# Unread products ahead of and between PE's first four transposes, orders planned anew, and a last output tile in two halves

## The chip, the core and the metric

The kernel runs on one core of one Trainium2 chip. The metric is the device time of one execution in microseconds (us). The engines are called PE (matrix products, with PEld for its weight loads), DVE (vector), ACT (scalar), POOL and SP; DMA transfers are issued from the queues of SP, ACT and POOL. PE writes into eight banks of 128 x 512 fp32 sums, called `acc` here.

## The reference

```python
# attention: q, k, v are [8, 8, 576, 64]; bias_table is [32, 8]
scores = (1/sqrt(64)) * q @ k^T + bias_table[bucket(|i - j|)]
attn   = exp(scores - max) / sum
x      = (attn @ v), heads side by side          # [4608, 512]
# feed-forward
h   = x @ w_in                                   # w_in [512, 2048]
g   = h + sin(alpha * h)**2 / (alpha + 1e-9)
out = g @ w_out                                  # w_out [2048, 512], out [4608, 512] fp32
```

## The kernel before, in words

There are eight batch elements t of 576 tokens, with eight heads each, taken as four pairs p. For each element, PE makes transposed scores (tasks `T t.p.wh`: query half w, key half h; `R`, `L` and `S` hold the rest rows and tail keys of several pairs at once), ACT takes their exponential (L1228, L1233, L1192), and DVE multiplies the part near the diagonal by the exponential of the bias (the "band", L1256, L1238, L1242, L1198), which is held as a Toeplitz array `toep`. PE then forms `attn @ v` with a column of ones for the sums (`av`, L1266 and L1276), DVE divides (`norm`, L1286, L1287), and the result is transposed into `xT`: by PE and a copy for element 0 (`turn_x`, L1300, copies `x0.p.w`), by DMA for the others.

k and q of elements 0 and 1 (and q of element 2) come in natural layout and are transposed on PE with an identity: 64-column tiles, two side by side ("cols" shape). Pair 0 of element 0 comes in four pieces (k and q, half 0 and 1), each loaded in fp32, cast (L991, L993), transposed (`turn_half`, L1135, six transposes) and copied (`half_copy`, L1145, L1147). The other pairs come by DMAs on POOL's queue and are transposed whole (`turn`, L1155, twelve transposes; copies L1163 on ACT, L1165 on DVE). All products that use 64 of 128 rows ("rows"), 64 of 128 columns ("cols"), or both ("quad") are different tile shapes of PE; the rest are "full".

The bias goes through a small product with the table (`bias_sub`, L1075), an exponential (L1079), four products (`bias_mm`, L1088), a copy (`bias_copy`, L1093) and then DMAs that write `toep` (L1103); POOL's `mask` copies follow.

The feed-forward part is cut into nine blocks of 480 to 576 tokens and 16 units each: four products (`in b.f`, L1325), a sine on ACT (L1332), a square on ACT (L1337) or DVE (L1339), and the sum on DVE (L1353). The 36 output tiles of 128 tokens are made in pairs of tiles, each of 16 products with w_out (`mo`, L1368), evicted by a copy on ACT (L1305) or DVE (L1307), and stored by SP (L1378), 256 KB each. Some of the `mo` work is done in the "rows" shape (`OPT["rows"]`), to stand next to score products without a change of shape.

Every piece of work is a `_Task` with an engine and an assumed duration. `_graph` (L425) makes them, and `_Plan.run` (L182) walks them in time. The order of each engine is fixed by hand-over: `LINE` (L361) lists task numbers, engine by engine, and each engine takes its tasks in exactly that order. `OPT["scalar"]` names the copies, squares and evictions that go to ACT instead of DVE. `_Plan.filled` (L311) can put products that nobody reads (`fill`, L1124, into a free bank, from the array `blank` of ones) ahead of the k-th PE task, spread from 1.1 us or the task before; `FILLS` is empty before the change, so none are made. The planner's durations for PE are those at full pace throughout.

POOL's queue takes its loads in order: a load that waits (for instance `load_vt` of element 2, which waits until element 0's `av` products have read the buffer) holds all behind it.

Of the kernel before, what the change touches and what calls it, by code (L numbers as in the profile page):

```python
# [10 lines left out]
F32 = mybir.dt.float32  # L11
# [89 lines left out]
class _Task:  # L101
    __slots__ = ("eng", "dur", "emit", "deps", "prio", "lat", "take", "seq", "sn", "name",
                 "m_in", "m_out", "pipe", "pkt", "flow", "start", "end", "idx", "got", "wait", "low", "alt")

    def __init__(self, eng, dur, emit, deps=(), prio=0.0, lat=0.0, take=(), seq=None, name="",
# [9 lines left out]
        self.low = 8  # L115
        self.alt = None
# [3 lines left out]
class _Plan:  # L120
    HOP = 0.06
    LAT = {"PE": 0.17, "ACT": 0.1, "DVE": 0.09, "POOL": 0.1}
    SWITCH = {"PE": 0.096, "ACT": 1.3}
    START = (0.5, 2.0)
# [57 lines left out]
    def run(self):  # L182
# [23 lines left out]
        while n:  # L206
            moved = False
            nxt = None
            for e, cand in pool.items():
# [61 lines left out]
                dur = t.dur  # L271
                if t.m_in is not None:
                    if mode.get(e, t.m_in) != t.m_in:
                        dur += self.SWITCH[e]
                    if t.m_in != t.m_out:
                        dur += self.SWITCH[e]
                    mode[e] = t.m_out
# [83 lines left out]
LINE = """  # L361
# [57 lines left out]
"""  # L419


FILLS = ()


def _graph(K, opt):  # L425
# [74 lines left out]
    for g in range(4):  # L500
        b_mm.append(add("PE", 0.35, None, deps=[b_sel] + b_mm[:1], prio=opt["p_bias"],
                        take=[] if g else [(1, s_users)]))
        b_mm[g].emit = lambda g=g: K.bias_mm(g, tag(b_mm[0]))
# [927 lines left out]
```

## Time and profile before

| | us |
|---|---|
| runs | 382.05, 381.51, 380.55 (median 381.51) |
| profiled execution | 382.92 |
| its span | 381.1 |
| first transpose on PE (L1135) | 4.56 |
| first exponential of scores (L1228) | 7.67 |
| first band product on DVE (L1256) | 18.36 |
| first feed-forward product (L1325) | 35.00 |
| last copy of an output tile (L1305) | 377.53 to 378.13 |

Times of instructions are from the start of the span. A row of instructions in order of time has its start, its length, engine, line, operation, output <- inputs and count, and in brackets the idle time of the engine before it with what ended that. A row of the chain of waits has start, length and what ran. A row of a group ends with busy time, mean ns of one, and idle time before.

### The profile page before, as it was taken

The page shows a single profiled execution, that of the slowest core. Times are in us where ns is not written, and L with a number is a line of the kernel's source. Part 1 is how long each engine was busy: PE and PEld are TensorE (multiplying, and loading weights), DVE is VectorE, ACT ScalarE, POOL GpSimd, SP SyncE. Part 2 cuts the span into 40 slices and gives each one's busy share as a digit, 9 for nine tenths or more (in the row PEclk, how much of TensorE's full clock was granted, in tenths as well). Part 3 has the DMA queues.
Part 4 walks back from the last instruction along what each step waited for, and adds up shares of the span by engine and source line. Part 5 has one row for each costly group of instructions (what it writes and reads, how often), then busy time and mean ns, then how long its engine had stood idle before and what let it go on. Part 6 is the DMA issues. An engine that isn't in the chain of part 4 may idle for free.

```text
span 381.1 us, 9520 instructions
## 1 busy us (share of the span) xinstructions
PE 369.9 (97%) x3939; PEld 201.3 (53%) x3939; DVE 268.3 (70%) x635; ACT 314.2 (82%) x419; POOL 88.2 (23%) x105
## 2 busy tenths in 40 slices
PE   4999999999999999999999999999999999999996
PEld 3566445756454556464655465546655545444442
DVE  4686988949964996579748974696569869668402
ACT  4788999899999999999999899997998686557311
POOL 8874651180028201910000008300000000000000
PEclk9999999999999999999999999999999999999999
DMA  8999999499939996997392049941710110210005
GB/s 158 203 157 153 176 186 125 81 148 148 173 82 147 162 158 82 183 157 167 43 182 79 3 96 154 108 67 23 160 58 17 37 37 19 72 57 3 0 2 220
DMA packets 148172, 40.82 MB, mean 107 GB/s; under 512 B 134416, under 2 KB 143456, under 8 KB 148128
## 3 DMA queue, kind: packets, MB, share of 16 engines
q0 software_dynamic: 96656, 18.45, 61.0%
q1 hardware_dynamic: 50768, 21.22, 27.8%
q8 instruction: 31, 0.51, 0.6%
q10 hardware_dynamic: 704, 0.53, 0.6%
q14 instruction: 13, 0.11, 0.1%
HBM read 36.94 MB, written 15.93 MB: 139 GB/s over the span
## 4 chain that ended last, share of the span: by engine, by line
PE 86%; DVE 5%; ACT 3%; DMA 3%; issue 1%; POOL 1%; ACTq 0%; POOLq 0%
PE acc L1368 31%; PE acc L1325 29%; PE acc L1276 10%; PE acc L1220 8%; PE acc L1266 3%; DVE g L1353 2%; ACT u L1228 2%; PE acc L1155 2%; DMA v<-in_v_dram 2%; DMA xT<-in_k_dram 2%; PE acc L1179 2%; PE acc L1210 1%; PE acc L1184 1%; DVE s L1339 1%; DVE xp L1287 1%
## 5 line engine op out<-in xcount | busy, mean ns | idle before, releaser
L1368 PE MATMUL acc<-w_out,g 128*128 128x512 f16 (+1 forms) x744 | 148.0, 378 | 0.6 <-DVE touched L1173 0.5
L1325 PE MATMUL acc<-xT,w_in 128*128 128x512 f16 (+2 forms) x640 | 134.7, 358 | 0.1
L1228 ACT ACTIVATE u<-acc 128x1024 f16<-128x1024 f32 x128 | 123.6, 1038 | 8.0 <-PE acc L1220 6.9
L1332 ACT ACTIVATE s<-acc,alphaT 128x512 f16<-128x512 f32 (+2 forms) x144 | 94.1, 684 | 24.4 <-PE acc L1325 18.2
L1353 DVE SCALAR_TENSOR_TENSOR g<-s,inv_a,acc 128x512 f16<-128x512 f16 (+4 forms) x176 | 107.5, 647 | 9.5 <-ACT s L1337 7.9
L1325 PEld LDWEIGHTS <-w_in 128*128 128x128 f16 x640 | 58.0, 98 | 66.1 <-issue 2.3
L1368 PEld LDWEIGHTS <-g 128*128 128x128 f16 (+1 forms) x744 | 51.2, 96 | 50.7 <-issue 8.4
L1256 DVE TENSOR_TENSOR u<-u,toep 128x1024 f16<-128x1024 f16 (+1 forms) x128 | 59.1, 487 | 26.6 <-ACT u L1228 26.5
L1035 POOL DMA_DIRECT2D v<-in_v_dram x32 | 33.3, 1116 | 91.8 <-PE acc L1276 85.1
L1220 PE MATMUL acc<-qT,kT 64*128 64x256 f16 x512 | 48.1, 285 | 0.5 <-DVE kT L1165 0.5
L1276 PE MATMUL acc<-v,u 128*128 128x65 f16 x1024 | 45.6, 195 | 0.1
L1337 ACT ACTIVATE s<-s 128x512 f16<-128x512 f16 (+2 forms) x70 | 43.2, 630 | 1.2
L1276 PEld LDWEIGHTS <-u 128*128 128x128 f16 x1024 | 41.5, 99 | 4.2 <-issue 0.2
L1307 DVE COPY outs<-acc 128x512 f32<-128x512 f32 x27 | 18.4, 687 | 27.7 <-PE acc L1368 27.2
L1339 DVE TENSOR_TENSOR s<-s 128x512 f16<-128x512 f16 (+2 forms) x74 | 30.2, 419 | 10.2 <-ACT s L1332 10.2
L1220 PEld LDWEIGHTS <-kT 64*128 64x128 f16 x512 | 22.0, 96 | 28.7 <-issue 16.3
L1287 DVE TENSOR_TENSOR xp<-acc,rden 128x256 f16<-128x256 f32 (+1 forms) x64 | 31.4, 491 | 2.4
L1266 PE MATMUL acc<-vt,ut 128*128 128x130 f16 x128 | 28.6, 224 | 0.0
L1041 POOL DMA_DIRECT2D vt<-in_v_dram x16 | 13.3, 832 | 51.8 <-PE acc L1179 27.3
L1305 ACT ACTIVATE outs<-acc 128x512 f32<-128x512 f32 x9 | 5.3, 603 | 18.4 <-PE acc L1368 18.4
L1228 ACT ACTIVATE ut<-acc 128x1024 f16<-128x1024 f32 x16 | 16.5, 1029 | 2.6 <-PE acc L1179 2.0
L1286 DVE RECIPROCAL rden<-acc 128x4 f32<-128x4 f32 (+1 forms) x64 | 11.8, 185 | 9.6 <-PE acc L1276 9.2
(70 smaller groups left out, 231.7 us busy)
## 6 DMA issues: line engine op xcount, KB each, us to landing
out_dram<-outs SPq DMA_DIRECT2D x36, 256.0 KB, 2.5
v<-in_v_dram POOLq DMA_DIRECT2D x32, 128.0 KB, 7.4
staged_k<-in_k_dram POOLq DMA_DIRECT2D x6, 576.0 KB, 11.1
staged_q<-in_q_dram POOLq DMA_DIRECT2D x5, 576.0 KB, 12.9
w_in<-in_moe_w_in_dram POOLq DMA_DIRECT2D x4, 512.0 KB, 8.8
w_out<-in_moe_w_out_dram POOLq DMA_DIRECT2D x4, 512.0 KB, 10.1
xT<-in_q_dram POOLq DMA_DIRECT2D x11, 144.0 KB, 6.5
xT<-in_k_dram POOLq DMA_DIRECT2D x7, 144.0 KB, 6.2
```

Of the source, the lines that this page charges most:

```text
L1220: self.nc.tensor.matmul(out=s[:, o:o + 256], lhsT=self.kT[t % 2][r, p, 128 * c:128 * c + 128], rhs=self.qT[t % 2][r, p, 256 * w:256 * w + ...
L1228: self.nc.scalar.activation(out=c["u"], in_=c["s"], func=AF.Exp, scale=0.125)
L1256: self.nc.vector.tensor_tensor(out=io, in0=io, in1=m, op=ALU.mult)
L1266: nc.tensor.matmul(out=c["av"][:, 130 * j:130 * j + 130], lhsT=tail, rhs=vt[:, p, :], start=True, stop=True, skip_group_check=True)
L1276: nc.tensor.matmul(out=c["av"][:, 130 * j + 65 * a:130 * j + 65 * a + 65], lhsT=l, rhs=vv[:, ch, 2 * p + a, 0:65], start=False, stop=True, ...
L1287: self.nc.vector.tensor_tensor(out=self.ap(x, 256 * w, [[64, n], [1, 64]]), in0=self.ap(av, 0, [[65, n], [1, 64]]), in1=self.ap(r, 0, [[1, ...
L1325: self.nc.tensor.matmul(out=c["h"][:, x:y], lhsT=self.w_in[:, j, 128 * f:128 * f + 128], rhs=self.xT[:, j, lo + x:lo + y], start=(j == 0), ...
L1332: self.nc.scalar.activation(out=c["s"], in_=c["h"], func=AF.Sin, scale=self.alphaT[:, f:f + 1])
L1337: self.nc.scalar.activation(out=c["s"], in_=c["s"], func=AF.Square)
L1339: self.nc.vector.tensor_tensor(out=c["s"], in0=c["s"], in1=c["s"], op=ALU.mult)
L1353: self.nc.vector.scalar_tensor_tensor(out=o, in0=c["s"][:, x:y], scalar=self.inv_a[:, f:f + 1], in1=c["h"][:, x:y], op0=ALU.mult, op1=ALU.add)
L1368: self.nc.tensor.matmul(out=c["mo"][i], lhsT=self.g[tau // 4][r, f, at:at + 128], rhs=self.w_out[r, f, :], start=i not in c["began"], stop ...
```

## The change

**Fills.** `FILLS` becomes ((0, 16),): sixteen unread products of 128 x 128 by 256 columns stand ahead of PE's first task. `fill` gets a "cols" form: two products of 64 columns, side by side. `warm_up` makes five such pairs behind the first k half's transpose, on which the second q half's transpose depends, and five behind that, on which the second k half's transpose depends. All later `turn`s of the first two elements, the first four score products and the first bias product depend on these ten. None stand later.

**Planner.** Each PE task gets a `cold` duration, used while the planned time is under `low_clock` = 6.5 us; changes of shape cost twice as much there. ACT's table load is counted as a task that emits nothing.

**Orders.** `LINE`, `OPT["rows"]` and `OPT["scalar"]` are new. What they say for the start, and in whole:

| | before | after |
|---|---|---|
| first four transposes on PE | k0, q0, k1, q1 | q0, k0, 5 pairs, q1, 5 pairs, k1 |
| then on PE | T0.0.00, T0.0.01, bias_sub, both turns of pair 1, bias_mm | T0.0.00, bias_sub, T0.0.01, T0.0.11, a turn of pair 1, bias_mm |
| ACT, behind the bias exponential | two T, bias_copy | two T, bias_copy |
| DVE ahead of the first band | six turn copies of element 0, one of element 1, alpha's three steps | six turn copies of element 0 |
| last of those six | load 7 of POOL's queue (pair 3, q) | load 10 (pair 2, k) |
| turn copies of element 1 on ACT ahead of the first sine | none | two |
| x copies of element 0 on ACT / DVE | 6 / 2 | 4 / 4 |
| turns of element 1 on PE ahead of in0.0 | 3 | 4 |
| places of w_in's quarters 0, 1, 2, 3 on POOL's queue | 20, 22, 27, 26 | 26, 17, 31, 35 |
| place of the first load there that waits for element 0's `av` | 30 | 33 |
| changes of tile shape along PE's tasks | 143 | 135 |
| squares / evictions on ACT | 70 / 9 | 75 / 8 |

**Last tile.** Of the last pair of output tiles, the second is made in two halves of 256 columns: 16 products, eviction (on DVE) and a store of 128 KB for each half.

```diff
-FILLS = ()
+FILLS = ((0, 16),)
+COLD = dict(turn_half=(0.22, 0.38), turn=(0.4, 0.48), qkT=(0.22, 0.42), qkR=(0.23, 0.43),
+            qkL=(0.43, 0.62), qkS=(0.12, 0.24), turn_x=(0.2, 0.27))
...
-                dur = t.dur
+                low = e == "PE" and now < self.LOW
+                dur = t.cold if low and t.cold else t.dur
+                switch = self.SWITCH[e] * (2 if low else 1) if t.m_in is not None else 0.0
...
+    add("ACT", 1.28, lambda: None, prio=-7.9, name="table")
...
+    def warm_up(n, behind):
+        some = []
+        for _ in range(n):
+            a = add("PE", 0.107, None, deps=[behind], prio=-9.45, take=[(1, [])], mode="cols", name="warm")
+            a.take[0][1].append(a)
+            a.emit = lambda a=a: K.fill("cols", tag(a))
+            some.append(a)
+        warm.extend(some)
+        return some
...
-            a = add("PE", 0.4, None, deps=[T_nat[t][p][kind], t_id], prio=opt["p_t1"][0] if t else -1,
+            a = add("PE", 0.4, None, deps=[T_nat[t][p][kind], t_id] + warm, prio=opt["p_t1"][0] if t else -1,
...
-                need = [halves[0][half], halves[1][w]]
+                need = [halves[0][half], halves[1][w]] + warm
...
+    def last_tile(cell, tau, users, first):
+        ou = []
+        for half in range(2):
+            ms = []
+            for f in range(0, NF, 4):
+                m = add("PE", 4 * 0.1092, None, prio=opt["p_mo"], mode="full", name=f"end{half}.{f}",
+                        deps=[T_wout[f // 4], first] + G_done[NBLK - 1][f:f + 4])
+                m.emit = lambda half=half, f=f: K.moe_half(cell, half, tau, range(f, f + 4))
+                ms.append(m)
+            ev = either(f"evict{tau}.{half}", 0.36, 0.38, lambda act, half=half: K.evict_half(cell, half, act),
+                        deps=ms, prio=opt["p_ev"], take=[] if half else [(outr, ou)])
+            users.append(ev)
+            ou.append(add("SP", 0.35, lambda half=half: K.store_half(cell, half, tau), deps=[ev],
+                          pipe=0.25, prio=-1))
...
+                for a, n, b in opt["warm"]:
+                    some = warm_up(n, turned[a])
+                    if b:
+                        turned[b].deps += some
+                b_mm[0].deps += warm
...
+    for t in plan.tasks:
+        if t.eng == "PE":
+            t.cold = COLD.get(t.name.rstrip("0123456789."), (t.dur, 2 * t.dur))[1]
+            if t.name[:2] == "av":
+                t.cold = 1.37 if t.name[-1] == "1" else 1.0
+    plan.LOW = opt["low_clock"]
...
+    warm=(((0, 0), 5, (1, 1)), ((1, 1), 5, (0, 1))), low_clock=6.5
...
     def fill(self, mode, bank):
-        r = slice(64 * (bank % 2), 64 * (bank % 2) + 64) if mode == "rows" else slice(0, 128)
-        self.nc.tensor.matmul(out=self.acc[:, bank, 0:256], lhsT=self.blank[r, 0:128],
-                              rhs=self.blank[r, :], start=True, stop=True)
+        for a in range(2 if mode == "cols" else 1):
+            r = slice(64 * (bank % 2), 64 * (bank % 2) + 64) if mode == "rows" else slice(0, 128)
+            c = slice(64 * a, 64 * a + 64) if mode == "cols" else slice(0, 128)
+            self.nc.tensor.matmul(out=self.acc[c, bank, 0:256], lhsT=self.blank[r, c],
+                                  rhs=self.blank[r, :], start=True, stop=True)
...
+    def moe_half(self, c, half, tau, fs):
+        at, n = 128 * (tau % 4), slice(256 * half, 256 * half + 256)
+        for f in fs:
+            self.nc.tensor.matmul(out=self.acc[:, c["bank"][1], n], lhsT=self.g[tau // 4][:, f, at:at + 128],
+                                  rhs=self.w_out[:, f, n], start=(half, "half") not in c["began"],
+                                  stop=True, skip_group_check=True)
+            c["began"].add((half, "half"))
```

More of the change, by code (lines that the diff above doesn't have):

```diff
@@ L102 @@
     __slots__ = ("eng", "dur", "emit", "deps", "prio", "lat", "take", "seq", "sn", "name",
-                 "m_in", "m_out", "pipe", "pkt", "flow", "start", "end", "idx", "got", "wait", "low", "alt")
+                 "m_in", "m_out", "pipe", "pkt", "flow", "start", "end", "idx", "got", "wait", "low", "alt",
+                 "cold")
     def __init__(self, eng, dur, emit, deps=(), prio=0.0, lat=0.0, take=(), seq=None, name="",
@@ L115, in __init__ @@
         self.low = 8
+        self.cold = None
         self.alt = None
@@ L123 @@
     SWITCH = {"PE": 0.096, "ACT": 1.3}
+    LOW = 0.0
     START = (0.5, 2.0)
@@ L500, in _graph @@
     for g in range(4):
-        b_mm.append(add("PE", 0.35, None, deps=[b_sel] + b_mm[:1], prio=opt["p_bias"],
-                        take=[] if g else [(1, s_users)]))
+        b_mm.append(add("PE", 0.06 if g else 0.18, None, deps=[b_sel] + b_mm[:1], prio=opt["p_bias"],
+                        take=[] if g else [(1, s_users)], name="bias"))
         b_mm[g].emit = lambda g=g: K.bias_mm(g, tag(b_mm[0]))
@@ L586, in feed_one @@
         return b
+    warm, turned = [], {}
+    def warm_up(n, behind):
[7 more added lines that the diff above has]
+        return some
     def turn_first():
@@ L594, in turn_first @@
                 a = add("PE", 0.22, None, deps=[first[kind][half], t_id], prio=-9.5, take=[(1, users)],
-                        mode="cols", name="turn_half")
+                        mode="cols", name=f"turn_half{kind}{half}")
                 a.emit = lambda a=a, cell=cell, kind=kind, half=half: K.turn_half(cell, tag(a), kind, half)
+                turned[kind, half] = a
                 if T_nat[2][0][kind] is not None:
@@ L770, in moe_out @@
         turns = [[], []]
-        rows = lambda f: n == 2 and (pair, f // 4) in opt["rows"]
+        split = taus[-1] == NT // 128 - 1
+        rows = lambda f: n == 2 and not split and (pair, f // 4) in opt["rows"]
         told = None
@@ L775, in moe_out @@
             if turn and n == 1:
+                break
+            if turn and split:
                 break
@@ L811, in moe_out @@
                     held.setdefault((b, j), []).append(m)
+        if split:
+            last_tile(cell, taus[1], users, first)
+            taus = taus[:1]
+            every = [m for m, _ in turns[0]]
         state["mo"] = m
@@ L1371, in moe_out, with evict_half, store_half @@
                 c["began"].add(i)
+    def moe_half(self, c, half, tau, fs):
[5 more added lines that the diff above has]
+            c["began"].add((half, "half"))
+    def evict_half(self, c, half, act):
+        if not half:
+            c["o", 1] = self.tp.tile([128, DM], F32, name="outs", tag="outs", bufs=3)
+        n = slice(256 * half, 256 * half + 256)
+        self.copy(c["o", 1][:, n], c["mo"][1][:, n], act)
+    def store_half(self, c, half, tau):
+        n = slice(256 * half, 256 * half + 256)
+        self.nc.sync.dma_start(out=self.out[128 * tau:128 * tau + 128, n], in_=c["o", 1][:, n])
     def evict(self, c, i, act):
```

27 lines of the change are left out of this document (14 added, 13 removed), and 114 rows, old and new, of the table LINE.

## The prediction, made before the changed kernel was run

> **What bounds the kernel now.** I read the page's busy shares first, then three stretches cut at the first exponential's wait, the first band product on DVE and the first feed-forward product, then the chain of waits from 8 to 36 us, and last the instructions in order of time on ACT, DVE, POOL and at the end. Columns of the stretches: length, then busy us (and instructions) of PE, weight loads, DVE, ACT and POOL, then granted clock, DMA share, GB/s.
>
> ```profile
> PE 369.9 (97%) x3939; PEld 201.3 (53%) x3939; DVE 268.3 (70%) x635; ACT 314.2 (82%) x419; POOL 88.2 (23%) x105
> PEclk9999999999999999999999999999999999999999
> 7.60:18.36 10.76, 9.40 (x133) 5.45 (x133) 5.64 (x11) 8.61 (x11) 8.56 (x14) 1.00 1.55 201
> 18.36:35.00 16.64, 16.01 (x292) 11.89 (x289) 14.44 (x42) 13.62 (x20) 9.46 (x16) 1.00 1.22 167
> 35.00:377.50 342.50, 341.51 (x3484) 182.01 (x3483) 244.57 (x566) 288.71 (x385) 63.26 (x61) 1.00 0.87 99
> ```
>
> From 35.0 us on PE is busy 341.51 of 342.50 us: the end is the start of the feed-forward work plus what PE has left. Ahead of that the chain shows a second thing.
>
> ```profile
> 8.39 0.69 PE acc L1155 x12
> 14.06 0.62 PE acc L1155 x12
> 33.58 0.38 PE acc L1155 x12
> 23.57 0.44 PE acc L1276 x8
> 26.84 0.34 PE acc L1276 x8
> 27.25 0.24 PE acc L1276 x8
> 18.15 0.54 PE acc L1220 x4
> 30.45 0.33 PE acc L1220 x4
> 35.00 12.25 PE acc L1325 x56
> ```
>
> Eight products of L1276 take 0.44 us at 23.57 and 0.24 us at 27.25; twelve transposes 0.62 and then 0.38. So PE runs at about half pace until 26.8 us, and at full pace after it. The clock row reads full all along, so that row does not show this state; the pace of equal instructions does. The pace rises 3.3 us after 23.57, where the dense run of L1276 begins. Before that PE was busy 9.40 of 10.76 us without rising.
>
> **The change, part by part.** *The fills.* The first transpose waits for a cast, and the operand of the fills is there early:
>
> ```profile
> 0.87 0.27 DVE L1011 MEMSET blank<- 128x256 f16 x1 [0.87 <-PEq L1415]
> 4.56 1.51 PE L1135 MATMUL acc<-ident,xT 96*64 96x96 f16 x24 [4.56 <-ACT xT L991]
> 7.60 0.18 ACT L1079 ACTIVATE e<-acc 128x8 f16<-128x8 f32 x1 [1.74 <-PE acc L1075]
> 7.67 1.94 ACT L1228 ACTIVATE u<-acc 128x1024 f16<-128x1024 f32 x2
> 10.30 0.50 ACT L1093 ACTIVATE e_sb<-acc 128x392 f16<-128x392 f32 x1 [0.69 <-PE acc L1088]
> ```
>
> A 512-column product takes 12.25/56 = 0.22 us at full pace, so 256 columns at half pace take 0.22 too, and 16 of them 3.5 us: from 1.14 to 4.65 us. They cover PE's 4.56 us idle wait and cost about 0.1; without that cover they would cost 3.5. No trace row shows a fill of two 64-column products. Its bounds are 0.11 (side by side, full pace) and 0.44 (in turn, half pace); I take 0.22 for the first five and 0.11 for the second, by the L1276 rows: 1.65 us for ten. With 24 transposes (two times 0.62) the four turns end near 7.5; T0.0.00, the small bias product and T0.0.01 follow, and the first exponential starts near 8.4 instead of 7.67: 0.7 late (bounds 0 and 2.5). The bias copy now stands behind two back-to-back exponentials, 8.4 + 1.94, so at 10.3 as before, and the bias loads behind it keep their time.
>
> *What full pace from 6.5 us is worth.* PE's groups up to 26.8 us would halve, some 9 us, but the feed-forward work can't start before ACT and DVE have finished element 0. ACT is busy 8.61 + 13.62 = 22.23 of the 27.40 us from 7.60 to 35.00. The new order gives it two turn copies in place of two x copies:
>
> ```profile
> L1163 ACT ACTIVATE kT<-acc 128x576 f16<-128x576 f16 x1 | 0.6, 634 | 0.0
> L1305 ACT ACTIVATE xT<-acc 128x320 f16<-128x320 f16 x3 | 1.2, 442 | 0.2 <-PE acc L1300 0.2
> ```
>
> That adds 2 x 0.63 - 2 x 0.42 = 0.4, so with no idle at all ACT is done at 7.60 + 0.7 + 22.23 + 0.4 = 31.0 us. DVE is tighter:
>
> ```profile
> 8.63 0.90 POOL L1035 DMA_DIRECT2D v<-in_v_dram  x1 [1.14 <-DMA xT<-in_k_dram]
> xT<-in_k_dram POOLq DMA_DIRECT2D x7, 144.0 KB, 6.2
> 16.45 1.42 DVE L1165 COPY qT<-acc 128x576 f16<-128x576 f16 x2 [0.30 <-PE acc L1155]
> 17.79 0.17 DVE L1119 COPY alphaT<-acc 128x16 f32<-128x16 f32 x1
> 18.19 0.25 DVE L1122 RECIPROCAL inv_a<-tmp_a 128x16 f32<-128x16 f32 x1
> 18.36 0.82 DVE L1256 TENSOR_TENSOR u<-u,toep 128x256 f16<-128x256 f16 x2
> 19.71 0.76 DVE L1165 COPY kT<-acc 128x576 f16<-128x576 f16 x1 [0.52 <-PE acc L1155]
> 34.33 0.61 DVE L1307 COPY xT<-acc 128x320 f16<-128x320 f16 x2
> ```
>
> In the new order the bands stand behind the six copies of element 0. The last of these waits for the tenth load on POOL's queue, issued near 9.5 (the ninth goes at 8.63), landing 6.2 later at 15.7, turned (0.2 to 0.4) and copied (0.76) by 16.8. Bands start near 17.0 instead of 18.36. Behind them DVE has its 14.44 us, less one turn copy (0.76), plus the other turn copy (0.71), alpha's steps (17.79 to 18.44, 0.6) and two x copies (0.61), which now stand inside: 15.6. Without idle it ends at 32.6; with all of its old idle (2.2 us) at 34.8. PE's slowness caused part of that idle; I keep 1.0 and take 33.6, against 35.0: **-1.4 us**. Ends: -4.0 if ACT alone limits, +0.7 if the late first exponential is passed on whole.
>
> *PE's work behind that point.* In the new order four turns of element 1 stand ahead of the first feed-forward product, not three: -0.4 (one turn of twelve, 0.38). The task order has 135 changes of PE's tile shape instead of 143.
>
> ```profile
> 61.60 0.54 PE acc L1220 x8
> 63.67 0.22 PE acc L1220 x4
> 65.24 0.33 PE acc L1220 x4
> ```
>
> Four products take 0.33 behind a change and 0.22 without: 0.1 each, **-0.8** (ends -0.9, and +1.5 if the new orders bring waits; the old ones leave PE 1.0 us idle in 342.5, so there is little to gain and something to lose). All other moves of the replan I cost at nothing, because PE's 99.7% covers them.
>
> *The last tile in halves.* PE's sum is the same (16 x 0.22 against 32 x 0.11).
>
> ```profile
> 376.47 2.01 SPq L1378 DMA_DIRECT2D out_dram<-outs  x3
> 377.53 0.60 ACT L1305 ACTIVATE outs<-acc 128x512 f32<-128x512 f32 x1 [0.61 <-PE acc L1368]
> L1307 DVE COPY outs<-acc 128x512 f32<-128x512 f32 x27 | 18.4, 687 | 27.7 <-PE acc L1368 27.2
> ```
>
> The last eviction goes from ACT's 0.60 to half of DVE's 0.69 with its fixed part, some 0.4: -0.2. The last store, half the bytes, gains between 0 and 0.5; I take 0.25. Together **-0.45** (ends -0.8 and 0).
>
> *Sum:* -1.4 - 0.4 - 0.8 - 0.45 = -3.05. Against the profiled execution, 382.92 us (its span of 381.1 and 1.8 around it), that is 379.9. That execution lies 1.4 above the median of the runs, 381.51, from which it is **378.4**.
>
> **The rivals.** *A. The pace falls back.* After 7 us PE has little dense work: for ACT's 0.97 us per exponential (1.94 for two) it needs 0.22. Nothing in this trace shows full pace held through such a stretch, and the rows from 7.60 to 18.36 show that scores and transposes don't raise it. Then 10 to 27 us runs at half pace, PE bounds the start as now, and the late first exponential stays: +0.7 - 1.65 = -0.95, 380.6. For it: those rows. [...]
>
> *B. The pace never rises early.* The dense run of fills is as long (3.5 us) as the run from 23.57 to 26.84, which just sufficed. If it fails, ten pairs cost 2.2 to 4.4 at half pace, the first exponential is about 2 us late: +2 - 1.65 = +0.35, 381.9. This is the case that the change doesn't do what it says. [...]
>
> *C. ACT, not DVE, sets the start.* If DVE's bands pack without idle behind earlier copies: -4.0 - 1.65 = -5.65, 375.9. Against: DVE is already 87% busy there.
>
> *D. The weights come late (slower).* Positions on POOL's queue: the first quarter of w_in moves from 20th to 26th, and the last quarter from 26th to behind the wait that ends here at 33.63:
>
> ```profile
> 18.10 0.77 POOL L1046 DMA_DIRECT2D w_in<-in_moe_w_in_dram  x1
> 23.72 1.51 POOL L1046 DMA_DIRECT2D w_in<-in_moe_w_in_dram  x2
> 33.63 0.63 POOL L1041 DMA_DIRECT2D vt<-in_v_dram  x1 [6.86 <-PE acc L1276]
> DMA to landing us min/median/max: 6.5/8.8/10.1
> staged_q<-in_q_dram POOLq DMA_DIRECT2D x5, 576.0 KB, 12.9
> ```
>
> The landing row is w_in's. The first quarter, issued at 23.7, lands at 32.5 to 33.8: it just fits. The last, issued about 1.4 earlier than 33.63 plus two issues (0.63 and 0.77), at 33.6, is needed after twelve units of 4 x 0.22, at 44.1. At 10.1 it is in time. A transfer of that size took 12.9 where the queue was full; at 16 it lands at 49.6, PE stands 5.5 us: +5.5 - 3.05 = +2.45, 384.0. It decides from a landing of 13.6 us on. Against: only two loads of its size stand directly ahead.
>
> **How the numbers follow.** Forecast 0.50, A 0.18, B 0.07, C 0.13, D 0.12. I predict 378.4; its own range, from DVE's bounds and the replan's, is 376.6 to 380.3. The range over cases is 375.5 to 383.2: it takes in C, A and B, and leaves out most of D. A measurement of this kernel tells about 0.5% (1.9 us) from no change, so faster means below 379.6 and slower above 383.4. Faster: 0.43 of the forecast's 0.50, all of C and a little of A, 0.58. Same: the rest of the forecast (0.07), most of A and B and a mild D, 0.30. Slower: 0.12.
>
> **What would show it.** Right: twelve transposes of L1155 take about 0.4 us from 8 us on, the first L1325 starts between 32.5 and 34.5, DVE has under 1.5 us idle between its first band and that point, PE is over 99% busy after it, and the last copy is some 0.4 us. A shows as groups of 0.62 again after some point before 20 us; B as no 0.38 before that; C as a start near 31; D as PE idle on a w_in transfer near 44. I am wrong if the first L1325 starts after 35, or if the time behind it grows by over 1 us.

## The result, and the profile after

| | before | after |
|---|---|---|
| median of the runs, us | 381.74 (380.55 to 383.08, 6 runs) | 385.76 (384.66 to 387.82, 6 runs) |
| ratio | | 1.0108, 95% interval 1.0076 to 1.0141 |
| profiled execution, its span | 382.92, 381.1 | 385.68, 383.9 |
| first exponential / first band / first feed-forward product | 7.67 / 18.36 / 35.00 | 8.05 / 17.2 / 35.94 |
| end of the last product on PE to the span's end | 3.6 | 3.1 |

The change costs 4.0 us (1.1%) where 3 were forecast as a gain. The page of the changed kernel, busy shares and clock row, then the two stretches of the start and the one from the first feed-forward product to the last product:

```profile
PE 371.4 (97%) x3999; PEld 205.6 (54%) x3999; DVE 266.7 (69%) x631; ACT 318.2 (83%) x425; POOL 88.4 (23%) x105
PEclk9669999999999999999999999999999999999999
7.60:18.36 10.76, 7.98 (x149) 5.21 (x149) 5.68 (x10) 8.10 (x10) 8.53 (x15) 0.73 1.61 193
18.36:35.00 16.64, 15.07 (x277) 11.50 (x272) 14.00 (x41) 14.00 (x19) 11.66 (x19) 0.76 1.13 153
35.94:380.80 344.86, 340.99 (x3498) 183.58 (x3496) 243.16 (x562) 292.16 (x390) 60.17 (x57) 1.00 0.84 100
```

The clock row, all nines before, now has two sixes. In the first stretches the granted clock is 0.73 and 0.76 where it read 1.00. (Before, it read 1.00 in both, although eight products of L1276 took 0.44 at 23.57 and 0.24 at 27.25; the row shows the fall here, and did not show the slow pace there.) In the last stretch PE is idle 344.86 - 340.99 = 3.87 us; before it was 342.50 - 341.51 = 0.99.

Between the first band product and the first feed-forward product DVE is busy and waits as follows (a stretch, then two rows of its waits: total, times, longest):

```profile
17.24:35.94 18.70, 17.13 (x311) 12.85 (x310) 15.60 (x46) 15.45 (x20) 13.57 (x22) 0.76 1.18 155
DVE rden L1346 <- PE acc L1336: 1.5, 3, 0.9
DVE xT L1367 <- PE acc L1360: 0.5, 1, 0.5
```

The start on PE in order of time, then pieces of the chain of waits (start, length, what ran), then two stretches:

```profile
4.74 0.69 PE L1195 MATMUL acc<-ident,xT 96*64 96x96 f16 x12
9.70 0.78 PE L1215 MATMUL acc<-ident,xT 96*64 96x96 f16 x24 [0.18 <-DMA xT<-in_q_dram]
12.16 0.45 PE L1215 MATMUL acc<-ident,xT 96*64 96x96 f16 x12 [1.68 <-DMA xT<-in_q_dram]
...
13.77 0.69 PE acc L1215 x12
23.21 0.44 PE acc L1336 x8
26.84 0.24 PE acc L1336 x8
36.01 0.54 PE acc L1385 x2
...
12.00:16.00 4.00, 3.16 (x64) 2.33 (x66) 1.51 (x2) 2.19 (x4) 2.94 (x6) 0.58 1.60 211
24.00:28.00 4.00, 4.00 (x74) 3.06 (x72) 2.46 (x9) 3.05 (x4) 4.00 (x7) 0.71 0.91 113
```

Twelve transposes take 0.69 at 4.74, half of 0.78 at 9.70, so the pace did rise early, and 0.69 again at 13.77, so it has fallen. A mean clock of 0.58 in 12 to 16 us is full to 12.6 and 0.50 behind it; 0.71 in 24 to 28 is 0.50 up to 26.3. Eight attention products (L1336) take 0.44 at 23.21 and 0.24 only at 26.84, about where they did before the change (27.25). PE's idle rows behind that point, then DVE's rows that go with the first and the last of them:

```profile
217.85 1.02 PE L1385 MATMUL acc<-xT,w_in 128*128 128x512 f16 x4 [0.41 <-DVE g L1413]
242.79 1.46 PE L1385 MATMUL acc<-xT,w_in 128*128 128x512 f16 x6 [1.91 <-DMA xT<-xp]
380.20 0.60 PE L1436 MATMUL acc<-w_out,g 128*128 128x256 f16 x4 [0.57 <-DVE outs L1367]
...
216.56 0.46 DVE L1128 COPY kd<-kT 64x256 f16<-64x256 f16 x2 [0.71 <-DMA kT<-staged_k]
379.72 0.42 DVE L1367 COPY outs<-acc 128x256 f32<-128x256 f32 x1 [1.39 <-PE acc L1436]
380.83 0.42 DVE L1367 COPY outs<-acc 128x256 f32<-128x256 f32 x1 [0.69 <-PE acc L1436]
```

At 217.85 the row names DVE, but DVE had itself stood 0.71 us for a transposed k (L1121, a DMA transpose on SP's queue): its sums came late, and PE's banks with them. At 242.79 PE waits for x transposes directly. At 380.20 the last four products wait for the first half's eviction, as both halves of the last tile are in one bank (e5, with two banks, has no such wait).

### The profile page after: what moved, and what is told of

It reads as the page before. It is cut to its first block, busy times and chain, and to the rows that moved or that the text cites. A ratio compares the mean times of both kernels' runs of the same rounds, so it can differ in the third digit from the quotient of the medians.

```text
span 383.9 us, 9642 instructions
## 1 busy us (share of the span) xinstructions
PE 371.4 (97%) x3999; PEld 205.6 (54%) x3999; DVE 266.7 (69%) x631; ACT 318.2 (83%) x425; POOL 88.4 (23%) x105
## 4 chain that ended last, share of the span: by engine, by line
PE 86%; DMA 6%; DVE 2%; ACT 2%; POOL 2%; issue 1%; SPq 0%; DVEq 0%; POOLq 0%
PE acc L1428 30%; PE acc L1385 30%; PE acc L1336 10%; PE acc L1280 8%; DMA xT<-xp 3%; PE acc L1326 3%; DMA xT<-in_q_dram 2%; PE acc L1215 2%; PE acc L1239 1%; DMA kT<-staged_k 1%; PE acc L1270 1%; PE acc L1244 1%; PE acc L1436 1%; POOL xT L1088 1%; ACT u L1288 1%
## 5 line engine op out<-in xcount | busy, mean ns | idle before, releaser
L1428 PE MATMUL acc<-w_out,g 128*128 128x512 f16 (+1 forms) x736 | 144.6, 378 | 0.7 <-DVE touched L1233 0.7
L1385 PE MATMUL acc<-xT,w_in 128*128 128x512 f16 (+2 forms) x640 | 135.0, 358 | 2.5 <-DMA xT<-xp 2.1
L1385 PEld LDWEIGHTS <-w_in 128*128 128x128 f16 x640 | 58.1, 98 | 68.6 <-issue 4.2
L1428 PEld LDWEIGHTS <-g 128*128 128x128 f16 (+1 forms) x736 | 50.0, 96 | 48.9 <-issue 9.5
L1397 ACT ACTIVATE s<-s 128x512 f16<-128x512 f16 (+2 forms) x75 | 45.7, 625 | 1.3
L1336 PE MATMUL acc<-v,u 128*128 128x65 f16 x1024 | 45.4, 195 | 0.0
L1336 PEld LDWEIGHTS <-u 128*128 128x128 f16 x1024 | 41.3, 98 | 4.2
L1367 DVE COPY outs<-acc 128x512 f32<-128x512 f32 (+1 forms) x29 | 19.0, 668 | 29.0 <-PE acc L1428 26.1
L1100 POOL DMA_DIRECT2D vt<-in_v_dram x16 | 12.2, 830 | 97.3 <-PE acc L1336 93.6
L1399 DVE TENSOR_TENSOR s<-s 128x512 f16<-128x512 f16 (+2 forms) x69 | 28.2, 420 | 8.4 <-ACT s L1392 8.0
L1326 PE MATMUL acc<-vt,ut 128*128 128x130 f16 x128 | 28.6, 223 | 0.0
L1293 ACT ACTIVATE ur<-acc 128x1024 f16<-128x1024 f32 x16 | 16.6, 1035 | 0.5 <-PE acc L1270 0.3
```

The costliest lines, as they stand in the source:

```text
L1326: nc.tensor.matmul(out=c["av"][:, 130 * j:130 * j + 130], lhsT=tail, rhs=vt[:, p, :], start=True, stop=True, skip_group_check=True)
L1336: nc.tensor.matmul(out=c["av"][:, 130 * j + 65 * a:130 * j + 65 * a + 65], lhsT=l, rhs=vv[:, ch, 2 * p + a, 0:65], start=False, stop=True, ...
L1385: self.nc.tensor.matmul(out=c["h"][:, x:y], lhsT=self.w_in[:, j, 128 * f:128 * f + 128], rhs=self.xT[:, j, lo + x:lo + y], start=(j == 0), ...
L1397: self.nc.scalar.activation(out=c["s"], in_=c["s"], func=AF.Square)
L1428: self.nc.tensor.matmul(out=c["mo"][i], lhsT=self.g[tau // 4][r, f, at:at + 128], rhs=self.w_out[r, f, :], start=i not in c["began"], stop ...
```

## The experiments

"Waits" below are PE's idle times ahead of feed-forward products (L1385) behind the first of them. Unless said otherwise the kernels compute the reference. Ratios are to the kernel before, measured beside each. Medians come from several rounds, and over these the median of the kernel before went from 381.74 to 382.49 us. So a difference between kernels of two rounds is uncertain by some 0.7 us, and the ratios are the better guide. e13 to e16 and e19 are single executions.

### What the unread products and the held pace are worth at the start

*e1: the pace held.* 59 more unread products behind the first sixteen, spread over PE's idle times (the expectation says 62). The output of this kernel differs from the reference; only its times are used.

```diff
-FILLS = ((0, 16),)
+FILLS = ((0, 16), (25, 2), (26, 14), (28, 7), (30, 2), (32, 2), (34, 4), (36, 5), (37, 6),
+         (38, 6), (39, 5), (40, 4), (42, 2))
```

> The changed kernel with 62 further unread products of 256 columns put ahead of later PE tasks, where PE stood idle between 9 and 22 us. Theory 1 (two separate losses: the pace falling back at 12.6 us, and waits that the new orders carry behind the first feed-forward product): the granted clock stays full from 7 to 27 us, the first feed-forward product starts between 33.0 and 34.5 instead of 35.94, the wait for the x transpose near 240 us and the one in the last tile stay, and the time is 383 to 384.5. Theory 2 (one loss: orders made for a fast PE meet a slow one, and all later waits follow from that): the later waits vanish too and the time is under 380.5. If the clock falls all the same, time as of the changed kernel, 385 to 387.

*e2: the sixteen products alone, with the orders of before.*

```diff
-FILLS = ()
+FILLS = ((0, 16),)
```

> The kernel before with the sixteen unread products ahead of its first transpose and nothing else of the change. Theory 1: the pace rises near 5 us and falls back between 9 and 14 us; the first feed-forward product starts between 34.3 and 35.2 and the time is 380.5 to 382 (before: 381.7). Theory 2: the same. A third theory, that the fills themselves cost (they end at 4.8 and so push the transposes): 382.5 or more.

*e3: the new orders without any unread product* (e14 and e16 are the same kernel).

```diff
-FILLS = ((0, 16),)
+FILLS = ()
...
-            a.emit = lambda a=a: K.fill("cols", tag(a))
+            a.emit = lambda: None
```

> The changed kernel without any of its unread products, its orders and its last tile kept. Theory 1: PE at half pace to 26 us, first feed-forward product at 36 to 37.5, the later waits as in the changed kernel, time 385.5 to 388. Theory 2: later waits grow with the slower start, 387 or more. If the fills themselves cost, it is faster than the changed kernel: 383 to 385.

*e7: only the ten pairs left out* (the second of these two edits).

> The changed kernel without the ten pairs of unread products between the first four transposes; the sixteen ahead of the first one stay. If the sixteen are what raises the pace too early, so that it falls back and is low in the run of L1336: first feed-forward product at 35.5 to 36.2 as in the changed kernel, and 385 to 386. If the ten pairs (1.0 us on the path to the first exponential, and the late loads behind it) are what costs: first feed-forward product near 34.5, no wait near 240 us, and 383 as without any unread products.

| | median, us | ratio (95%) | first feed-forward product |
|---|---|---|---|
| e1 | 383.05 | 1.0029 (1.0005 to 1.0053) | 34.2 |
| e2 | 381.56 | 0.9979 (0.9961 to 0.9997) | 34.0 |
| e3 | 382.70 | 1.0017 (0.9989 to 1.0045) | 34.3 |
| e7 | 384.31 | 1.0060 (1.0037 to 1.0082) | 35.1 |

Stretches of e1 (with a piece of its chain of waits, L1187 being an unread product), of e2 (with two rows of its PE in order of time) and of e3, columns as above (PE's busy time first, granted clock third from the right):

```profile
10.00:15.00 5.00, 4.86 (x114) 4.05 (x113) 2.88 (x4) 3.88 (x6) 2.91 (x6) 1.00 1.74 199
20.00:25.00 5.00, 5.00 (x82) 3.31 (x81) 4.60 (x16) 4.80 (x7) 4.71 (x9) 1.00 1.12 130
...
11.54 1.53 PE acc L1187 x28
```

```profile
6.05 0.32 PE L1135 MATMUL acc<-ident,xT 96*64 96x96 f16 x6 [0.28 <-ACT xT L991]
8.41 0.63 PE L1155 MATMUL acc<-ident,xT 96*64 96x96 f16 x12 [0.27 <-DMA xT<-in_q_dram]
...
7.00:8.00 1.00, 0.66 (x14) 0.60 (x14) 0.19 (x1) 0.49 (x2) 0.52 (x2) 1.00 1.28 178
8.00:9.00 1.00, 0.73 (x24) 0.48 (x18) 0.00 (x0) 1.00 (x2) 1.00 (x2) 0.76 1.26 190
20.00:25.00 5.00, 4.43 (x62) 3.08 (x60) 4.91 (x15) 4.36 (x5) 4.83 (x8) 0.50 1.14 178
```

```profile
20.00:25.00 5.00, 4.48 (x61) 3.14 (x61) 4.86 (x18) 4.62 (x6) 4.77 (x9) 0.66 0.92 99
```

With the pace full all through (e1) the first feed-forward product comes at 34.2. With half pace from 8.5 to 25.6 (e2, the old orders) it comes at 34.0, and at 34.3 in e3, where the four bias products (L1147) take 508 ns each in the mean, against 340 in the changed kernel, and where the clock of 0.66 in 20 to 25 us is 3.4 us at 0.50. So holding the pace in this way brings no early start. What a held pace alone would bring isn't shown: in e1 some 6.4 us of unread products, such as the row at 11.54, stand on the chain between 11 and 23 us.

e3 went against its first two theories, which had 36 to 37.5 for the start and later waits as in the changed kernel. It has neither, and is faster than even the third said. Without the ten pairs the changed kernel is 1.4 faster (384.31 against 385.76), although the execution of e7 that was profiled, its slowest, has a wait of 2.0 near 218 us. Without the sixteen as well it is another 1.6 faster; the intervals of e7 and e3 overlap, so the split between the two isn't settled. All 26 cost the new orders 3.1 us (3.5 by the ratios, 1.0108 against 1.0017, whose intervals are apart), while on the old orders the sixteen alone gain 0.7 (382.28 beside it to 381.56, the interval reaching to 0.9997). What the sixteen do to the start thus doesn't explain what they cost.

### The last tile

*e5: the second half in a bank of its own.*

```diff
+            if half:
+                own = []
+                ms[2].take = [(1, own)]
+                for m in ms[:2] + ms[3:]:
+                    m.deps.append(ms[2])
...
-out=self.acc[:, c["bank"][1], n]
+out=self.acc[:, c["second"].got[0] if half else c["bank"][1], n]
```

> The changed kernel, with the second half of the last tile in a bank of its own, so that its last four products need not wait for the first half's eviction. If that wait (0.6 us) is on the path to the end: the wait is gone, the second copy starts 0.5 to 0.6 earlier, and the time falls from 385.8 to 385.2. Rival: the end is set by the stores, which then collide; the time stays at 385.8.

384.56, ratio 1.0064 (1.0034 to 1.0094), 1.2 below the changed kernel's median of another round. The last products now run in one piece:

```profile
376.13 3.22 PE L1442 MATMUL acc<-w_out,g 128*128 128x256 f16 x28
```

The wait of 0.57 is gone, as expected. What that is worth in time isn't settled: the interval overlaps that of the changed kernel (1.0076 to 1.0141), and the later waits also differ, 1.9 us in this execution against 2.5.

### The waits near 218 and 242 us

*e4: one of POOL's loads of element 7 earlier* (stage k ahead of vt), to thin out what the x transposes meet near 242 us.

```diff
+    line=_moved(_line(LINE), 1407, 1416)
```

> The changed kernel with one load moved on POOL's queue: the staging of k for element 7, second in a burst of twelve loads at 232 us, goes one place up, ahead of the load that waits there, and so is issued near 161 us. Theory 1: the x transposes near 235 us land in under 4 us instead of 7.7, the 1.9 us wait at 240 us is gone or under 0.7, and the time is 1.2 to 2.2 under the changed kernel's 385.8. Theory 2: the wait is a consequence of the late start and shows at another load or place; the time stays within 0.6 of the changed kernel.

384.59, ratio 1.0064 (1.0039 to 1.0089), first feed-forward product at 36.2, waits of 1.4 at 218.8 and 1.1 at 243.0 us. The wait was not removed; the 1.2 us below the changed kernel's median are within the spread of that kernel's own runs (384.66 to 387.82). Inconclusive.

*e8 and e9: a late start.* Sixteen unread products ahead of attention's first product (L1326, before L1266), in the new orders without the other products (place 42, shown), and in the kernel before (place 34). From here to e11, and in e19, an unread product also goes ahead of a task planned for the same time; the diffs show the places alone.

```diff
-FILLS = ()
+FILLS = ((42, 16),)
```

> The changed kernel without its 26 unread products, but with 16 ahead of the first product of L1326, so that attention's last part and the first feed-forward product come some 1.7 us later (36.0) with the same orders. Theory 'late start' (the orders hold only as long as the start is near the planned one, and a late one brings the later DMA wait): the wait for an x transpose near 240 us comes back with 1 to 2 us, and the time is 382.7 + 1.7 + 1.9 = 386.3. Theory 'fixed' (the delay is passed on and nothing more): no such wait, 384.4.

> The kernel before with the same 16 unread products ahead of its first product of L1266: first feed-forward product near 36.7 instead of 35.0. If the old orders pass a delay on one to one: 381.7 + 1.7 = 383.4. If they too are upset by a late start: 385 and a DMA wait behind 200 us. If the delay is taken up again later: below 382.5.

e8: 386.31, ratio 1.0113 (1.0083 to 1.0143), first feed-forward product at 36.1, a wait of 1.7 at 219 and 0.2 at 242 us. e9: 385.33, ratio 1.0101 (1.0070 to 1.0132), but in its profiled execution (383.12, its fastest) the first feed-forward product comes at 34.0: there the products only brought the full pace forward (eight attention products take 0.41 in order of time at 23.98, where the changed kernel's take 0.65 at 23.00). So e9 says nothing about delays.

*e10 and e11: the same sixteen right ahead of the first feed-forward product* (places 68 and 57), where the pace is full.

> The changed kernel without its 26 unread products, but with 16 of them right ahead of the first feed-forward product, where the pace is full: 16 x 0.11 = 1.7 us on PE, and attention ahead of it stays as it was. Theory 'late start' (the new orders hold only near the planned start): 382.7 + 1.7 + 1.5 to 1.9, about 386, with PE waits of 1 to 2 us near 218 or 242 us. Theory 'passed on': 384.4, waits as without the delay. If the later work has slack that takes it up: below 384.

> The kernel before with the same 16 unread products right ahead of its first feed-forward product. If its orders pass a delay on one to one: 381.8 + 1.7 = 383.5. If they too turn a late start into later waits: 385 and more. If they are the more tolerant ones, as the theory of too tight new orders has it, this kernel loses 1.7 or less and the one with the new orders more than 3.

e10: 385.19, ratio 1.0103 (1.0063 to 1.0143); e11: 383.34, ratio 1.0036 (1.0018 to 1.0054). Rows of e10, and its list of PE's waits behind the start (total, times, longest):

```profile
35.65 1.90 PE L1187 MATMUL acc<-blank 64*128 64x256 f16 x16
37.48 1.90 PE L1385 MATMUL acc<-xT,w_in 128*128 128x512 f16 x8
...
PE acc L1385 <- DMA xT<-xp: 0.4, 1, 0.4
```

The latest start so far, 37.48, and no wait at 218 or 242 us. So a late start alone need not bring the later waits. That it never does isn't shown: e8 has one near 219 us, and two of e10's six runs, without profiles, took 388.5 and 388.7. Both orders pass the delay on: 1.3 in the old ones (383.34 against 382.04 beside it; 1.8 expected from the row), 2.5 in the new ones against e3's median (3.3 by the ratios), over six runs that spread by 4 us.

*e13 to e16: the changed kernel and e3, twice more each.*

> The changed kernel once more, for a second profiled execution. If its late start belongs to it: first feed-forward product at 35.5 to 36.3 again. If the waits near 218 and 242 us follow from that start: 1.5 to 2.5 us of them again. If they come by chance from one execution to the next (a DMA transpose that lands a little later): they may be gone, and the span is then the first feed-forward product + 345.7 (what stood behind that product in the runs without such waits).

> The changed kernel without its 26 unread products once more. If its early start belongs to it: first feed-forward product at 34.0 to 34.6, and no later wait above 0.5 us. If chance rules: a first feed-forward product up to 36, or a wait of 1 to 2 us near 218 or 242 us, as in its two runs of 385.2 to 385.4.

> As the run before with this kernel: a third execution; the same two theories. In all of them the span should be the first feed-forward product + 345.7 + the later waits, within 0.4 us.

> As the run before with this kernel: a third execution; the same two theories, and the same sum of first feed-forward product + 345.7 + later waits.

| execution | first feed-forward product | wait near 218 / 242 | all waits | span | span less both |
|---|---|---|---|---|---|
| changed kernel | 35.9 | 0.4 / 1.9 | 2.5 | 383.9 | 345.5 |
| e13 | 35.6 | 0.8 / 1.4 | 2.2 | 383.1 | 345.3 |
| e15 | 36.2 | 0.5 / 0.7 | 1.6 | 383.1 | 345.3 |
| e3, no products | 34.3 | none / none | 0.2 | 380.0 | 345.5 |
| e14, no products | 34.8 | none / none | 0 | 379.9 | 345.1 |
| e16, no products | 36.2 | none / none | 0 | 381.7 | 345.5 |
| before | 35.0 | none / none | 0 | 381.1 | 346.1 |
| e2, old orders | 34.0 | none / none | 0.3 | 380.2 | 345.9 |

So the span is the first feed-forward product, plus the waits, plus a fixed rest. The rest is 0.4 to 1.0 shorter with the new orders. The waits stand in all three executions with the unread products and in none of three without, and e16 has the late start without them. The wait near 218 us doesn't go with products at the start alone, though: it also stands in e7 (2.0), e8 (1.7) and e19 below (1.0), and not in e1 or e10. The start itself varies by 1.9 us from execution to execution without the products; e16 has its pace low for longer than e3:

```profile
20.00:25.00 5.00, 4.20 (x52) 2.92 (x52) 4.90 (x17) 4.64 (x7) 4.71 (x9) 0.64 0.87 97
25.00:30.00 5.00, 5.00 (x86) 4.07 (x85) 2.91 (x10) 2.59 (x4) 4.57 (x7) 0.68 0.97 135
```

What stands ahead of the wait at 242 us, on SP's queue (length: SP's own issue time), first in the changed kernel, then in e16. Both transposes start 189 us behind the first feed-forward product:

```profile
225.42 2.91 SPq L1121 DMA_TRANSPOSE qT<-staged_q  x1
229.01 7.24 SPq L1353 DMA_TRANSPOSE xT<-xp  x3
```

```profile
225.31 2.39 SPq L1121 DMA_TRANSPOSE qT<-staged_q  x1
228.37 6.89 SPq L1353 DMA_TRANSPOSE xT<-xp  x3
...
240.17 6.00 PE L1385 MATMUL acc<-xT,w_in 128*128 128x512 f16 x27
```

The transpose of q needs 2.91 us of SP where it needs 2.39 in e16; the x transposes behind it and a store start 0.64 later (229.01 against 228.37) and reach further into POOL's burst of loads (from 232.04), to 236.25 against 235.26. Every execution of these orders has that burst. Over all executions, SP needs 2.56 to 3.13 us there in the six that have just the 16 products and ten pairs (the changed kernel, e4, e5, e13, e15, e17), all with a wait of 0.7 to 2.4 at 242 us, and 2.05 to 2.39 in the eight others with the new orders (e1, e3, e7, e8, e10, e14, e16, e18), none with a wait above 0.5 there. The transpose of k near 211 us divides them in the same way: 2.99 to 4.26 in the six, 2.27 to 2.74 in the eight.

*e19: the length of PE's program without the start.* As e3, with 36 matrix instructions (as many as the 16 products and ten pairs are) ahead of the first feed-forward product.

```diff
-FILLS = ()
+FILLS = ((68, 36),)
```

> The changed kernel without its 26 unread products, but with as many matrix instructions (36) right ahead of the first feed-forward product, so that PE's program is as long as in the changed kernel and the start of it as without. In the executions with the wait near 242 us, SP needs 2.6 to 3.1 us to issue the transpose of q that stands ahead of the x transposes there; in those without it, 2.05 to 2.4 us. If the length of the program is what makes that issue slow: 2.6 to 3.1 us and a wait of 0.7 to 2.4 us. If it is what the unread products do at the start: 2.05 to 2.4 us and no wait above 0.5 us. The delay itself is 3.9 us: first feed-forward product at 38 to 40, and the span that + 345.7.

One execution: first feed-forward product at 39.8, waits of 1.0 and 0.5, span 386.8, which less both is 345.5.

```profile
229.76 2.95 SPq L1121 DMA_TRANSPOSE qT<-staged_q  x1
...
222.18 1.02 PE L1385 MATMUL acc<-xT,w_in 128*128 128x512 f16 x4 [1.04 <-DVE g L1413]
245.70 4.48 PE L1385 MATMUL acc<-xT,w_in 128*128 128x512 f16 x20 [0.49 <-DMA xT<-xp]
```

The slow issue (2.95) is back without any product at the start. That speaks for the longer program, not for what the products do to the pace; but it is one execution, the wait at 242 us is the smallest of its kind, and e1, whose program is longer still, has 2.31.

The DMA queues during the issue of that transpose of q show one difference. First the changed kernel's, 225.42 to 228.33, then all of e16's, 225.31 to 227.70 (packets, MB, share of 16 engines):

```profile
q1 hardware_dynamic: 669, 0.17, 58.3%
q8 instruction: 1, 0.02, 2.5%
```

```profile
q1 hardware_dynamic: 794, 0.20, 43.3%
```

A transfer of the queue that the page calls `q8 instruction` falls into this issue in all seven executions with a slow one (the six and e19), and in none of the eight others, e1 among them. So the length of PE's program may act by where these transfers fall. That this is what slows the issue is not shown: no run moves such a transfer by itself.

*e17 and e18: two places of slack.* DVE's copies of k's tail (L1128) two sums later, with the last half tile's own bank; e18 without the unread products as well.

```diff
+    line=_moved(_line(LINE), 1209, 1134)
```

> The changed kernel with the last half tile's own bank, and with DVE's two copies of k's tail (L1128, element 6) two sums later in DVE's order, so that DVE no longer reaches them before the transposed k has landed. If the new orders' lack of slack there is what makes a slow DMA transpose stop PE near 218 us: that wait (0.4 to 0.8 in the three profiles of the changed kernel) is gone, and 384.6 of the own-bank run falls to 384.0. The wait near 242 us (another transfer) stays at 0.7 to 1.9. If the wait only moves to the next task of DVE: 384.6 and an idle time of the same length.

> The run before without the 26 unread products. If these are what costs, whatever is done to the tail and to the wait at 218 us: near 382.0 (382.7 less the last tile's 0.6), first feed-forward product between 34.3 and 36.2, no later wait above 0.5 us; that is 2 us under the run before. If the later waits come by chance: 383 to 384, with a wait at 242 us.

e17: 384.10, ratio 1.0051 (1.0028 to 1.0074); e18: 381.79, ratio 0.9981 (0.9959 to 1.0003). Waits of e17, then of e18:

```profile
PE acc L1398 <- DMA xT<-xp: 3.1, 2, 2.4
PE acc L1441 <- DVE touched L1246: 0.7, 3, 0.2
```

```profile
PE acc L1441 <- DVE touched L1246: 0.7, 3, 0.2
PE acc L1398 <- DMA w_in<-in_moe_w_in_dram: 0.4, 1, 0.4
```

With two places of slack the wait at 218 us is gone; the one at 242 us stands, longer than expected, and goes with the products. That pair of runs measures the unread products again, side by side and with intervals that are apart: 384.10 - 381.79 = 2.3 us.

### The best version

*e12: the orders of before, the sixteen products, and the last tile in halves with a bank each* (the options of before in the changed program, without pairs, the eight half-tile tasks last on PE).

> The kernel before with the sixteen unread products ahead of the first transpose, its own orders, and the last tile in halves with a bank for each half, all sixteen half products of it last on PE. The sixteen were worth 0.4 (381.56 in their own run); the halves should take 0.5 to 0.9 from the end: 380.6 to 381.1, faster than both kernels. Rival: the move of the last tile's products behind all others leaves PE waiting for evictions or banks: 381.6 or more.

381.39, ratio 0.9976 (0.9960 to 0.9991): faster than both kernels, by 0.2% over the one before, of which e2's sixteen products alone give 0.2%. The halves' 0.5 can't be told from these runs. (The expectation's 0.4 for the sixteen is 0.7 against the kernel before of the same round.) Its first feed-forward product came at 34.3, and the span less start and waits is 345.6 (345.9 in e2).

## Why the prediction was wrong

**Full pace from 6.5 us (-1.4).** The pace rose early, but fell back at 12.6 and was half until 26.3. This is rival A, whose place and rows were right: scores and transposes didn't hold the pace (a granted clock of 0.50 in 16 to 24 us). That it would hold through PE's gaps was the author's estimate; no row of before showed it. The fall came without a long gap: in the changed kernel the longest gap ahead of it is 1.68 us, in e2 the pace falls near 8.5 us with no gap above 0.3 us since 4.7, PE being busy 0.66 and 0.73 of the last two us ahead of it. Most of PE's rows in e2 from 4.7 to 9 us are transposes (48 of the 58 products up to 8.96 us). Whether the pace fell because of that kind of work, or because PE was simply not busy enough, isn't shown, as no run puts other work in their place.

**Start set by DVE at 33.6.** DVE's work was right: 17.24 for the first band (17.0 forecast) and 15.60 us busy behind it (15.6 forecast). What failed is "I keep 1.0" of idle: it is 18.70 - 15.60 = 3.1 us, of which 1.5 went by waiting for attention's products, on a PE at a mean clock of 0.76. With the pace held (e1) it is 1.6 (16.91 less 15.31 busy) and the start 34.2.

The step also set this gain against the start of a single execution, 35.00, and then took the sum from the median of the runs. That execution lies 1.4 above the median. By the fixed rest, 346.1, and 1.8 us around the span, a run at 381.7 starts its feed-forward part near 33.8 (an estimate; no profile of before shows it, but in e11's, with the old orders, PE is ready for it at 32.83 and then makes the sixteen unread products). Against that, the changed kernel's 35.6 to 36.2 are some 2 us late, not 0.9, and the forecast's 33.6 would have been a gain of only 0.2. So part of the gain was only that execution's own late start.

**"All other moves of the replan I cost at nothing, because PE's 99.7% covers them."** With it failed the price of the unread products, "about 0.1" for the sixteen and 0.7 at the first exponential for the pairs, with nothing behind the start. These two are the steps that failed most: the three executions have 1.6 to 2.5 us of waits there, more than the +1.5 kept as an end, and it takes both, as the new orders without the products (e3, e14, e16) have 0.2 at most, and so has e2 (0.3) with the sixteen on the old orders. PE's full row said that the old orders had slack for their DMA transposes, not that any order has. The cover was in the order itself: the old one has DVE copy k's tail with no wait, the new one reaches it 0.2 to 0.4 us early in its best executions, so a delay of that transfer goes through to PE near 218 us.

**Changes of shape and one turn ahead (-0.8, -0.4).** PE's busy time from the first feed-forward product to the last product is 340.99 against 341.51: -0.5, not -1.2. One turn is 0.38, so about 0.1 is left for the eight changes, not 0.8.

**The last tile (-0.45).** Right in what it named: from the last product to the span's end 3.1 instead of 3.6. The last copy takes 0.42 instead of 0.60 (-0.2 forecast), and from its end to the span's end it is 2.65 instead of 2.97 (-0.25 forecast, the author's estimate). Missed was a wait of 0.57 that the change adds: both halves share a bank, so the second half's last products stand behind the first eviction. The terms cancel; e5 shows the wait gone with a second bank.

**The rivals.** B and C didn't come: the pace rose, and the start is far from 31. D (w_in late) was worth 0.8 us in e1 and 0.4 in e18 near 46 us, and nothing in the changed kernel. A's 380.6 missed by 5 us because it took the other terms over whole, and the range failed for the same reason: its ends were set one case at a time, but a pace that falls back and new waits came together.

In sum, the forecast's span was 381.1 - 3.05 = 378.05, and the changed kernel's 383.9 is 5.85 longer: 2.34 at the start (35.94 instead of 33.6), 2.5 in waits where none were forecast, and 1.0 in the rest (345.5 instead of 378.05 - 33.6 = 344.45). The other 1.4 of the miss is the step from that execution to the median. Settled is that the unread products cost the new orders 2.3 to 3.5 us, so most of the 4.0 that the change loses; in the executions with a profile, 0.8 of it is in the start (means of 35.9 against 35.1) and the larger part in the later waits. Why a transpose issues more slowly 200 us later is open, and so is why the transpose of k takes 6.6 and 6.3 us to DVE's copy in e7 and e8, where its issue is short, against 4.5 to 4.8 in e1, e3, e10, e14 and e16.

## What to carry to other kernels

A gain at the start is worth what the next bound leaves of it: hold the state artificially once (e1) before planning orders around it, and see how much of the work that holds it stands on the chain itself. An engine that is 99.7% busy shows that its present order has slack at each transfer, not that another order has; see, for each wait on a transfer, how long before its landing the waiting engine arrives. Where one execution is the base of a sum, settle first whether its start is a typical one.

## What the runs showed of the hardware

In e2 the pace falls back near 8.5 us without a gap above 0.3 us since 4.7. The stretches at a clock of 0.50 at the start are 3.4 us long in e3 (a mean of 0.66 in 5 us), 6.8 in e16 (3.6 and 3.2, by 0.64 and 0.68), 13.7 in the changed kernel and 17.1 in e2, within 0.1 us of 1, 2, 4 and 5 times the first; e7 has 10.2 (0.73, 0.50 and 0.75 in 5 to 20 us) and another 3.4 (0.66 in 20 to 25). What sets these lengths isn't shown. Executions of one kernel differ in how much of attention's last part runs at half pace: 6.8 us in e16, with a start of 36.2, and 3.4 in e3, with 34.3; e14, with 34.8, has a mean clock of 0.996 over its span (e3 0.994, e16 0.991). That these stretches decide the start is a reading; no run moves them.

In e7 the pace also fell behind a single idle of 1.97 us in the middle of full work; the last row is e17's, with an idle of 2.40 us and no fall:

```profile
218.43 1.44 PE L1385 MATMUL acc<-xT,w_in 128*128 128x512 f16 x4 [1.97 <-DVE g L1413]
216.00:220.00 4.00, 2.03 (x8) 0.69 (x6) 2.78 (x6) 2.35 (x5) 0.00 (x0) 0.86 0.02 4
220.00:222.00 2.00, 2.00 (x6) 0.76 (x5) 1.97 (x5) 1.11 (x2) 0.00 (x0) 0.50 0.01 4
...
240.00:244.00 4.00, 1.60 (x13) 0.60 (x8) 3.10 (x7) 3.20 (x4) 1.24 (x2) 1.00 2.21 150
```

In e7 the wait of 1.97 us was followed by half pace (a clock of 0.50 in 220 to 222 us, 0.92 in 222 to 224), and the span less start and waits is 347.0 instead of 345.1 to 345.5: an idle of 2 us cost 3.5 to 3.9 there. The granted clock stayed at 1.00 after e17's 2.40 and after the changed kernel's 1.91 at 242 us, so the length of the gap alone doesn't tell.
